# fp64 weights decoded by two parametric ReLUs and one VectorE pass instead of one scaling and three VectorE passes, with the rows loaded from their third byte on and the first stage put in another order

## The chip, the cores and the metric

The kernel runs on one core of a Trainium2 chip. The metric is the device time of one execution in microseconds (us). TensorE is called PE here, VectorE DVE, ScalarE ACT, GpSimd POOL, and SyncE, which issues nearly all transfers, SP.

## The reference, cut to what matters

Three blocks follow one another: an attention over 32 memory slots per head (8 batches of 576 tokens, 8 heads of 64), a feed-forward block with a squared ReLU (512 to 2048 to 512), and a second one with a softmax-gated unit and a layer norm (512 to 1024 to 512).

```python
a = softmax(phi)                      # over the 32 memory slots
k_m, v_m = a^T k, a^T v               # per batch and head
attn = softmax(q k_m^T / 8)           # over the 32 slots
x = (attn v_m)                        # 4608 tokens x 512
h = maximum(x @ w_in, 0);  x = (s * h * h + b) @ w_out
h = x @ w_in2;  x = layer_norm(h * softmax(h)) * g_ln @ w_out2
```

The four weight matrices come as 64-bit floating point (their scale factor is a 64-bit number), everything else as 32-bit. No engine computes in 64 bits, so the kernel builds a 32-bit float out of the bits of every weight. The first block's w_in (512x2048) and w_out (2048x512) are 8 MB each in that form.

## The kernel before, in words

Tokens lie batch after batch. The eight batches n = 0..7 are worked off in halves j = 0, 1 of 288 tokens. From batch 1 on the products run as pairs of 16-bit pieces. Batch 0 is a stage of its own, called FIRST, because it runs while the weights of the first feed-forward block are still being loaded and decoded; its first half uses 32-bit products.

**FIRST is a list of steps written out by hand** (lines 33 to 54 before the change): each name is a call, and the order of the names is the order in which every engine gets its instructions. Each engine works strictly in that order and waits where an operand or a buffer is missing. The names that matter here:

- Lphi, Lkv, Lq, Lw, Lo: loads on SP's queue, of phi, of k and v, of q, of a piece of w_in, of a piece of w_out. A piece is 128 partitions by 1024 weights, 1 MB; w_in is eight pieces c.x (c is the quarter of 512 columns, x the half of the rows), w_out another eight.
- Ai/Ao, Ci/Co, PiX/PoX: the three decoding steps of a piece of w_in or w_out. Before the change Ai (line 281) reads the upper 32-bit word of each weight as a float and multiplies it by 2^-112 on ACT; Ci (lines 285 and 286) shifts left by three and puts the sign back, two DVE passes; PiX (line 1201) fetches three more bits from the lower word, one DVE pass. Bi/Bo (line 294) then sums the piece's squares or absolute values on ACT.
- qm, qo: q of two heads is transposed on PE (line 561) and copied out on ACT (line 573). km, ks, ko: the memory products of k and v (lines 472 and 497) and their normalization. mm, mv, mk: their transposes and copies.
- s0, s1, s2, s3, s6, at, aA: scores of two of the six token chunks (line 844), softmax on DVE and ACT (lines 856 to 877), transposes back on PE (line 906), copy on ACT (line 914).
- vm, vA/vD: v_m times a quarter of w_in (line 609) and the copy out of PSUM (line 919).
- g, gr, gs: first products of batch 0 (line 927, four 32-bit products of 288 columns a step), ReLU (line 1035) and square (line 944) on ACT. Before g can start, two chunks' at/aA and one quarter's vm/vA have to be done.
- y and Y: second products of batch 0 (lines 955 and 1106).

PSUM tiles named h (tq, kp, sp, wp, ta, tx, hp) share three buffers, so a product can also wait until ACT or DVE has emptied an earlier tile. KEEP (line 58) is a table of filler products on PE (line 163) that are put in front of a step and whose result is not used. After FIRST comes the loop over n = 1..7, whose first product is line 1024. The change does not touch that loop.

Of the kernel before, what the change touches and what calls it, by code (L numbers as in the profile page):

```python
# [28 lines left out]
REBIAS = 2.0 ** -112  # L29
# [35 lines left out]
def tile_mem_attention__moe_relu2__solu_ln(  # L65
# [15 lines left out]
    nc = tc.nc  # L81
# [15 lines left out]
    scale = 1.0 / float(D) ** 0.5  # L97

    const = ctx.enter_context(tc.tile_pool(name="const", bufs=1))
# [17 lines left out]
    xiv = const.tile([128, NT // GRP], FP32)  # L117
    nhalf = const.tile([128, 1], FP32)
    half = const.tile([128, 1], FP32)
    rsc = const.tile([128, 1], FP32)  # L120
    sb = const.tile([128, 2], FP32)
    s22 = const.tile([128, 1], FP32)
# [4 lines left out]
    iw = const.tile([128, KD], FP32)  # L127
# [3 lines left out]
    gl = const.tile([128, KF2], FP32)  # L131
# [91 lines left out]
    def pow2_scale(al, inv, tag="sc", w=1):  # L223
# [915 lines left out]
    raw_t, pk_t = {}, {}  # L1139

    def load_w_in(f, kp, t):
        src = w_in.bitcast(I32)[kp * 256:(kp + 1) * 256, f * 1024:(f + 1) * 1024]
        nc.sync.dma_start(
            out=t.rearrange("p k f w -> p k (f w)"), in_=src.rearrange("(k p) f -> p k f", p=128)
        )
        raw_t["in", f, kp] = t

# [3 lines left out]
    def load_w_out(d, x):  # L1151
        if x == 0:
            t = w_out_t[d].rearrange("p a k d -> p (a k d)").bitcast(I32)
        else:
            t = raw_p.tile([128, 2048], I32, tag="raw", name="raw")
        rows = w_out.bitcast(I32)[x * 1024:(x + 1) * 1024, d * 256:(d + 1) * 256]
        nc.sync.dma_start(
            out=t.rearrange("p (k d) -> p k d", k=8), in_=rows.rearrange("(k p) d -> p k d", p=128)
        )
        raw_t["out", d, x] = t.rearrange("p (a x w) -> p a x w", a=2, w=2)  # L1160

# [21 lines left out]
    def piece_abs(w, c, x):  # L1183
        if w == "o":
            at = (2 * c + x) % 4
            wt_t[c, x] = wt_s[:, at] if at < 3 else flat(r2_s)[:, 0:1024]
        decode_rebias(*piece(w, c, x))

    def piece_low(w, c, x, eng):
        decode_low(raw_t["in" if w == "i" else "out", c, x], eng)  # L1190

    def piece_bits(w, c, x):
        decode_shift(*piece(w, c, x))

    def piece_add(w, c, x):
        decode_add(*piece(w, c, x))
# [375 lines left out]
    with tc.manual_schedule():  # L1572
        make_identity(nc, ident)
        nc.vector.memset(ones, 1.0)
        nc.vector.memset(nhalf, -0.5)
        nc.vector.memset(half, 0.5)
        nc.vector.memset(c15, 2.0 ** -15)
# [105 lines left out]
```

## Time and profile before

| | |
|---|---|
| median of two runs | 1087.83 us (1087.77 to 1087.89) |
| the profiled execution | 1088.45 us, of which 1086.7 us are the span from the first to the last instruction |
| PE busy | 1058.0 us, 97% of the span |
| DVE, ACT, POOL busy | 766.1, 527.4, 170.7 us |
| moved by DMA | 129.22 MB |

The profiled execution is 0.62 us longer than the median of the runs, and 1.75 us of it lie outside the span. PE's 28.7 idle us are the difference of its busy time and the span. The page cuts the span into 40 slices of 27 us; PE's digits there begin 5, 7 and stand at 9 nearly everywhere after that, and the DMA digits begin 9, 8, 9 and then fall to 5.

### The profile page before, as it was taken

The page shows a single profiled execution, that of the slowest core. Times are in us where ns is not written, and L with a number is a line of the kernel's source. Part 1 is how long each engine was busy: PE and PEld are TensorE (multiplying, and loading weights), DVE is VectorE, ACT ScalarE, POOL GpSimd, SP SyncE. Part 2 cuts the span into 40 slices and gives each one's busy share as a digit, 9 for nine tenths or more (in the row PEclk, how much of TensorE's full clock was granted, in tenths as well). Part 3 has the DMA queues.
Part 4 walks back from the last instruction along what each step waited for, and adds up shares of the span by engine and source line. Part 5 has one row for each costly group of instructions (what it writes and reads, how often), then busy time and mean ns, then how long its engine had stood idle before and what let it go on. Part 6 is the DMA issues. An engine that isn't in the chain of part 4 may idle for free.

```text
span 1086.7 us, 20776 instructions
## 1 busy us (share of the span) xinstructions
PE 1058.0 (97%) x8439; PEld 698.6 (64%) x8439; DVE 766.1 (71%) x1499; ACT 527.4 (49%) x775; POOL 170.7 (16%) x141
## 2 busy tenths in 40 slices
PE   5799999989999999999999999999999999999998
PEld 4577777767777777777777777754444444444443
DVE  4799988768768767767767766467766666666662
ACT  3689754654553553663653655423333333333322
POOL 0000200130120130120120110023122222221221
PEclk9999999999999999999999999999999999999999
DMA  9894535524725625636625152125443443434325
GB/s 295 271 256 137 126 108 108 134 60 121 177 64 134 166 61 134 167 61 163 167 60 124 27 185 63 32 58 119 105 107 88 113 105 94 107 95 110 88 59 107
DMA packets 208607, 129.22 MB, mean 119 GB/s; under 512 B 137344, under 2 KB 196736, under 8 KB 208512
## 3 DMA queue, kind: packets, MB, share of 16 engines
q1 hardware_dynamic: 208368, 127.70, 45.9%
q8 instruction: 66, 1.08, 0.4%
q14 instruction: 29, 0.24, 0.1%
q10 hardware_dynamic: 112, 0.20, 0.1%
q0 software_dynamic: 32, 0.00, 0.0%
HBM read 71.83 MB, written 23.07 MB: 87 GB/s over the span
## 4 chain that ended last, share of the span: by engine, by line
PE 88%; DVE 4%; DMA 3%; ACT 2%; POOL 1%; issue 1%; SPq 0%; POOLq 0%; ACTq 0%; DVEq 0%
PE y L1106 29%; PE y L1510 17%; PE hp L1428 17%; PE hp L1024 14%; PE hp L927 3%; PE y L955 3%; PE kp L472 2%; DMA q_s<-in_q_dram 2%; PE wp L651 1%; PE sp L800 1%; DMA work<-in_moe_w_out_dram 1%; DMA wt_s<-in_v_dram 1%; PE wp L609 1%; PE tq L561 1%; POOL e L877 0%
## 5 line engine op out<-in xcount | busy, mean ns | idle before, releaser
L1106 PE MATMUL y<-g,w_out 128*128 128x288 f16 x2688 | 338.5, 286 | 0.0
L1106 PEld LDWEIGHTS <-w_out 128*128 128x128 f16 x2880 | 278.1, 98 | 85.4 <-issue 11.0
L1428 PE MATMUL hp<-w_t,xs 128*128 128x512 f16 x864 | 192.0, 379 | 0.0
L1510 PE MATMUL y<-w_t,lt 128*128 128x512 f16 x864 | 191.7, 379 | 0.0
L1024 PE MATMUL hp<-aT,vwt 128*128 128x288 f16 x1344 | 167.6, 286 | 3.9 <-ACT r L1035 3.9
L1024 PEld LDWEIGHTS <-vwt 128*128 128x128 f16 x1344 | 131.4, 98 | 37.8 <-issue 4.6
L1510 PEld LDWEIGHTS <-lt 128*128 128x128 f16 x864 | 84.6, 98 | 101.7
L1428 PEld LDWEIGHTS <-xs 128*128 128x128 f16 x864 | 84.5, 98 | 101.4
L1472 POOL TENSOR_TENSOR rstd<-ve,nhalf 128x1 f32<-128x1 f32 x36 | 52.6, 1462 | 332.8 <-DVE mv L1470 332.8
L1442 DVE TENSOR_REDUCE hmx<-hp 128x1 f32<-128x1024 f32 x36 | 44.1, 1224 | 84.1 <-PE hp L1428 84.1
L314 ACT ACTIVATE xs<-xt,xsc 128x512 f16<-128x512 f32 x36 | 25.9, 720 | 151.3 <-PE hp L1428 129.9
L1123 ACT ACTIVATE x<-y,bcol,cs 128x288 f32<-128x288 f32 x60 | 35.1, 586 | 109.4 <-PE y L1106 99.8
L1089 DVE TENSOR_TENSOR g<-r_s,g 128x576 f16<-128x576 f32 x112 | 85.3, 762 | 3.8
L1082 ACT ACTIVATE r_s<-r 128x576 f32<-128x576 f32 x112 | 76.6, 684 | 16.8 <-DVE g L1089 13.6
L1035 ACT ACTIVATE r<-hp 128x576 f32<-128x576 f32 x120 | 77.3, 644 | 13.9 <-PE hp L1024 6.9
L1009 DVE CAST g<-r_s 128x576 f16<-128x576 f32 x112 | 51.5, 460 | 24.4 <-ACT r_s L1082 24.2
L1449 ACT ACTIVATE e<-hp,nm,xiv 128x1024 f32<-128x1024 f32 x36 | 43.3, 1202 | 45.6 <-DVE nm L1444 45.6
L311 DVE TENSOR_REDUCE xmx<-x 128x1 f32<-128x288 f32 x64 | 28.8, 450 | 50.6 <-ACT x L1123 50.2
L1518 ACT ACTIVATE o<-y,io 128x512 f32<-128x512 f32 x36 | 24.7, 687 | 53.0 <-issue 40.5
L1486 DVE TENSOR_TENSOR nat<-so,nat 128x1024 f16<-128x1024 f32 x36 | 43.8, 1216 | 5.4 <-ACT nat L1481 5.4
L1465 DVE BATCH_NORM_STATS2 bs<-so 128x6 f32<-128x512 f32 x72 | 46.3, 685 | 1.3
L1460 DVE SCALAR_TENSOR_TENSOR so<-hp,sm,e 128x1024 f32<-128x1024 f32 x36 | 46.2, 1284 | 1.3
(242 smaller groups left out, 1194.2 us busy)
## 6 DMA issues: line engine op xcount, KB each, us to landing
x_d<-x SPq DMA_DIRECT2D x64, 144.0 KB, 2.0
xt<-x_d SPq DMA_DIRECT2D x36, 256.0 KB, 3.1
kv_s<-in_k_dram SPq DMA_DIRECT2D x31, 288.0 KB, 6.6
kv_s<-in_v_dram SPq DMA_DIRECT2D x31, 288.0 KB, 7.2
q_s<-in_q_dram SPq DMA_DIRECT2D x21, 288.0 KB, 4.7
phi_sb<-in_phi_dram SPq DMA_DIRECT2D x8, 576.0 KB, 4.9
out_dram<-o SPq DMA_DIRECT2D x23, 192.0 KB, 2.6
w_out<-in_moe_w_in_dram SPq DMA_DIRECT2D x4, 1024.0 KB, 16.0
```

The lines of the kernel that those rows point to most:

```text
L1009: nc.vector.tensor_copy(out=g_of(n, j, 0)[:, 2 * fp:2 * fp + 2, 0:BLK], in_=gt["r2", j, fp])
L1024: nc.tensor.matmul(out=hp[:, u, 0:BLK], lhsT=vt[:, pw, R, f * 128:(f + 1) * 128], rhs=aT[:, CJ * j:CJ * (j + 1), pa, R, :], start=(x == 0) ...
L1035: nc.scalar.activation(out=r, in_=gt.pop(("h", j, fp))[:, :, 0:BLK], func=ACTF.Relu, scale=scale)
L1082: nc.scalar.activation(out=r2, in_=r, func=ACTF.Square)
L1089: (nc.vector if eng == "D" else nc.gpsimd).tensor_tensor(out=g_of(n, j, 1)[:, fs, 0:BLK], in0=gt.pop(("r2", j, fp)), in1=g_of(n, j, 0)[:, ...
L1106: nc.tensor.matmul(out=y[:, 0:w], lhsT=w_out_t[d][:, pw, f, :], rhs=g_of(n, j, pg)[:, f, 0:w], start=(x == 0), stop=(x == len(steps) - 1),)
L1428: nc.tensor.matmul(out=hp[:, a, :], lhsT=xs[:, px, kk, :], rhs=wt[:, pw, kk, a * 512:(a + 1) * 512], start=(kk == 0 and px == 0 and pw == ...
L1442: nc.vector.tensor_reduce(out=mx, in_=hv, op=ALU.max, axis=AX)
L1460: nc.vector.scalar_tensor_tensor(out=so, in0=hv, scalar=sm[:, 0:1], in1=e, op0=ALU.mult, op1=ALU.mult)
L1465: nc.vector.bn_stats(out=bs[:, a, :], in_=so[:, a * 512:(a + 1) * 512])
L1472: nc.gpsimd.tensor_tensor(out=rstd, in0=ve, in1=nhalf, op=ALU.pow)
L1510: nc.tensor.matmul(out=y[:, 0:DM], lhsT=lt[:, pl, f, :], rhs=wt[:, pw, f, :], start=(x == 0), stop=(x == len(steps) - 1),)
```

## The change

The source of a weight's row is now read as 16-bit words, starting with the second one, so every row lacks its first two bytes and each weight lies two bytes lower in the piece. Its top 16 bits (sign, exponent, four bits of mantissa) are then the third half-word of its eight bytes. Ai became a parametric ReLU on ACT that reads that half-word as an integer, with a bias and a slope of 2^60 for negative numbers; Ci became a second one that writes integers, with another bias and a slope of 2^-60; together they put the exponent and the sign in place. PiX shifts by 13 instead of 29 and brings the other 19 bits. So ACT has two passes for a piece where it had one, and DVE one where it had three. One copy of two numbers went from DVE to ACT. FIRST has a new order, and KEEP a new table (42 fillers instead of 25).

```diff
-Lphi.0 phm.0 Lkv.00 pht.0 phd.0 Lkv.01 pho.0 phb.00 phe.00 km.00 Lkv.03 Lkv.02 ks.00 phb.01 phe.01 km.01 ks.01 ko.00
...
+Lphi.0 phm.0 pht.0 phd.0 Lq.00 pho.0 phb.00 Lq.01 qm.00 Lkv.03 qm.01 qo.00 phe.00 Lkv.00 qo.01 Lq.02 phb.01 Lkv.01
...
 KEEP = {
-    "pht.0": 3, "km.00": 3, "mm.0": 3, "qm.02": 2, "qm.03": 1, "s0.00": 1, "vap.0": 1, "s0.02": 1, "at.1": 9,
-    "pho.1": 1,
+    "pht.0": 3, "km.00": 1, "vap.0": 1, "qm.02": 6, "qm.01": 3, "qm.00": 6, "s0.00": 1, "pht.1": 4, "at.1": 4,
+    "at.0": 2, "g.01": 9, "g.05": 1, "at.2": 4,
 }
-    def decode_rebias(dst, raw):
-        nc.scalar.activation(out=dst, in_=raw[:, :, :, 1].bitcast(FP32), func=ACTF.Copy, scale=REBIAS)
-
-    def decode_shift(dst, raw):
-        di = dst.bitcast(I32)
-        nc.vector.tensor_scalar(out=di, in0=di, scalar1=3, scalar2=None, op0=ALU.logical_shift_left)
-        nc.vector.scalar_tensor_tensor(
-            out=di, in0=raw[:, :, :, 1], scalar=-0x80000000, in1=di, op0=ALU.bitwise_and, op1=ALU.bitwise_or,
+    def decode_knee(dst, raw):
+        nc.scalar.activation(
+            out=dst, in_=raw.bitcast(I16)[:, :, :, 2], func=ACTF.Prelu, bias=knee[:, 0:1], scale=1.0, alpha=2.0 ** 60,
+        )
+
+    def decode_place(dst, raw):
+        nc.scalar.activation(
+            out=dst.bitcast(I32), in_=dst, func=ACTF.Prelu, bias=knee[:, 1:2], scale=2.0 ** 19, alpha=2.0 ** -60,
         )
     def load_w_in(f, kp, t):
-        src = w_in.bitcast(I32)[kp * 256:(kp + 1) * 256, f * 1024:(f + 1) * 1024]
+        src = w_in.bitcast(I16)[kp * 256:(kp + 1) * 256, f * 2048 + 1:(f + 1) * 2048]
...
-        rows = w_out.bitcast(I32)[x * 1024:(x + 1) * 1024, d * 256:(d + 1) * 256]
+        rows = w_out.bitcast(I16)[x * 1024:(x + 1) * 1024, d * 512 + 1:(d + 1) * 512]
...
-            out=dst.bitcast(I32), in0=raw[:, :, :, 0], scalar=29, in1=dst.bitcast(I32),
+            out=dst.bitcast(I32), in0=raw[:, :, :, 0], scalar=13, in1=dst.bitcast(I32),
             op0=ALU.logical_shift_right, op1=ALU.bitwise_or,
...
-        nc.vector.tensor_copy(out=iw[:, 2 * d:2 * d + 2], in_=inv.to_broadcast([128, 2]))
+        nc.scalar.copy(out=iw[:, 2 * d:2 * d + 2], in_=inv.to_broadcast([128, 2]))
```

Three places show what the new order does; line numbers of the changed kernel are two higher from line 83 on (and six higher at the end of the file). On SP, the loads at the start of the program, before (phi_sb, kv_s, q_s are phi, k and v, q; wt_s holds one more of either; the tiles whose source is in_moe_w_in_dram receive w_in):

```order
L332 DMA phi_sb<-in_phi_dram 96x8x192
L357 DMA kv_s<-in_k_dram 96x2x384
...
L357 DMA kv_s<-in_v_dram 96x2x384
L1143 DMA raw_g<-in_moe_w_in_dram 128x2x1024
L1143 DMA raw<-in_moe_w_in_dram 128x2x1024
L1143 DMA raw_g<-in_moe_w_in_dram 128x2x1024
L366 DMA wt_s<-in_q_dram 96x2x384
L1143 DMA raw<-in_moe_w_in_dram 128x2x1024
L366 DMA q_s<-in_q_dram 96x2x384 x3
L332 DMA phi_sb<-in_phi_dram 96x8x192
```

and in the changed kernel:

```order
L334 DMA phi_sb<-in_phi_dram 96x8x192
L368 DMA q_s<-in_q_dram 96x2x384 x2
L359 DMA wt_s<-in_k_dram 96x2x384
L359 DMA wt_s<-in_v_dram 96x2x384
L359 DMA kv_s<-in_k_dram 96x2x384
L359 DMA kv_s<-in_v_dram 96x2x384
L368 DMA q_s<-in_q_dram 96x2x384
...
L368 DMA wt_s<-in_q_dram 96x2x384
L1145 DMA raw_g<-in_moe_w_in_dram 128x2x2047 x2
L1145 DMA raw<-in_moe_w_in_dram 128x2x2047 x2
```

All four pieces of q now go ahead of all w_in, where before four pieces of w_in went ahead of three of q. On PE, the same stretch of the changed kernel after the first filler products (tq is a transpose of q, kp the memory products, sp scores, ta a transpose of the softmax, wp the product with w_in, hp the first real product of batch 0):

```order
L423 MATMUL tx<-first 96x256
...
L563 MATMUL tq<-ident,q_s 64x96 x12
...
L563 MATMUL tq<-ident,q_s 64x96 x12
...
L563 MATMUL tq<-ident,q_s 64x96 x12
...
L474 MATMUL kp<-kv_s,phi_sb 32x128 x24
...
L563 MATMUL tq<-ident,wt_s 64x96 x12
L541 MATMUL tp<-ident,km 128x128 x2
...
L846 MATMUL sp<-kmT,qt_s 96x2x32 x24
```

Before, the memory products came first and each score product behind the transposes of all of q. Ahead of the three tq groups now stand 6, 3 and 6 fillers. On ACT, what stood between the first scaling of a piece and the first exponential before:

```order
L281 ACTIVATE w_in_t<-raw_g 128x2x512
L546 COPY first<-tp 64x128 x2
L281 ACTIVATE w_in_t<-raw 128x2x512
L550 COPY kmT<-tp 64x4x32 x2
L281 ACTIVATE w_in_t<-raw_g 128x2x512
L294 ACTIVATE junk,pk<-w_in_t 128x1024
L281 ACTIVATE w_in_t<-raw 128x2x512
L573 COPY qt_s<-tq 128x576 x3
```

and now, from the first parametric ReLU on:

```order
L283 ACTIVATE w_in_t<-raw_g,knee 128x2x512
L548 COPY first<-tp 64x128 x2
L288 ACTIVATE w_in_t<-w_in_t,knee 128x2x512
L865 ACTIVATE e<-e 96x512 x2
L283 ACTIVATE w_in_t<-raw_g,knee 128x2x512
L288 ACTIVATE w_in_t<-w_in_t,knee 128x2x512
L296 ACTIVATE junk,pk<-w_in_t 128x1024
L865 ACTIVATE e<-e 96x512
L283 ACTIVATE w_in_t<-raw,knee 128x2x512
L916 COPY aT_119<-ta 128x2x192
L288 ACTIVATE w_in_t<-w_in_t,knee 128x2x512
L296 ACTIVATE junk,pk<-w_in_t 128x1024
```

The exponentials of the scores and the copies that PE waits for now stand between the decoding passes of w_in, where before four pieces had been scaled ahead of the first exponential.

## Rows read from the trace of the kernel before

**Rows 1.** Windows by stage: start:end, length, busy us (instructions) per engine, clock, DMA.

```profile
0.00:50.00 50.00, 31.93 (x414) 24.18 (x415) 30.41 (x56) 22.56 (x34) 0.68 (x6) 1.00 1.00 306
50.00:110.00 60.00, 60.00 (x465) 45.27 (x464) 56.94 (x108) 55.30 (x84) 1.00 (x1) 1.00 0.66 181
...
150.00:1087.00 937.00, 926.08 (x7232) 599.20 (x7229) 640.41 (x1270) 424.60 (x624) 163.00 (x131) 1.00 0.43 106
```

**Rows 2.** Chain of waits, 0 to 200 us: start, us, what; xN counts two records a product.

```profile
12.18 17.10 DMA q_s<-in_q_dram
...
29.32 4.11 PE tq L561 x48
33.43 1.89 PE wp L609 x16
...
49.88 5.88 PE hp L927 x24
55.76 1.43 PE kp L472 x46
57.19 0.47 PE kp L497 x39
57.66 1.02 PE wp L609 x16
...
71.70 3.90 PE y L955 x16
...
150.66 11.78 PE hp L1024 x96
```

**Rows 3.** Timeline of PE, 0 to 62 us: start, us, what, count, idle before.

```profile
10.17 0.85 PE L163 MATMUL kp<-first 128*128 128x256 f16 x3
12.30 2.89 PE L472 MATMUL kp<-kv_s,phi_sb 96*32 96x128 f32 x48 [1.28 <-ACT phi_sb L449]
...
43.67 1.16 PE L163 MATMUL ta<-first 128*128 128x256 f16 x9
...
46.52 0.59 PE L421 MATMUL tx<-first 128*96 128x256 f32 x2
```

**Rows 4.** Timeline of ACT, 33 to 46 us.

```profile
38.36 1.07 ACT L294 ACTIVATE junk<-w_in_t 128x1024 bf16<-128x1024 f32 x1
...
39.55 1.06 ACT L294 ACTIVATE junk<-w_in_t 128x1024 bf16<-128x1024 f32 x1
...
42.33 0.63 ACT L863 ACTIVATE e<-e 96x512 f32<-96x512 f32 x1 [1.62 <-DVE e L858]
42.86 1.28 ACT L281 ACTIVATE w_in_t<-w_out 128x1024 f32<-128x1024 f32 x1
```

**Rows 5.** Groups by line and shape, DVE, 0 to 240 us: busy us, mean ns, idle.

```profile
L285 DVE TENSOR_SCALAR w_in_t<-w_in_t 128x1024 int32<-128x1024 int32 x8 | 5.5, 686 | 0.0
...
L286 DVE SCALAR_TENSOR_TENSOR w_in_t<-w_out,w_in_t 128x1024 int32<-128x1024 int32 x4 | 4.9, 1225 | 0.1
...
L1201 DVE SCALAR_TENSOR_TENSOR w_in_t<-w_out,w_in_t 128x1024 int32<-128x1024 int32 x4 | 4.8, 1219 | 0.0
```

**Rows 6.** The same view, ACT.

```profile
L1035 ACT ACTIVATE r<-hp 128x576 f32<-128x576 f32 x25 | 16.2, 647 | 3.6 <-PE hp L1024 1.7 <-PE hp L927 0.7
...
L314 ACT ACTIVATE w_out<-wt_s,sc 128x1024 f16<-128x1024 f32 x6 | 6.8, 1137 | 0.0
...
L1035 ACT ACTIVATE r<-hp,rsc 128x576 f32<-128x576 f32 x8 | 5.8, 725 | 0.2 <-DVE rsc L1039 0.2
...
L281 ACT ACTIVATE w_in_t<-w_out 128x1024 f32<-128x1024 f32 x4 | 4.7, 1181 | 0.0
...
L914 ACT COPY aT<-ta 128x384 f32<-128x384 f32 x3 | 1.4, 470 | 0.4 <-PE ta L906 0.4
```

**Rows 7.** Windows in which k, v, phi load, and in which w_in loads.

```profile
4.00:10.00 6.00, 1.34 (x4) 0.83 (x5) 2.58 (x5) 1.28 (x1) 0.00 (x0) 1.00 1.09 268
33.00:38.00 5.00, 4.30 (x46) 2.22 (x42) 0.19 (x1) 2.33 (x5) 0.00 (x0) 1.00 1.02 404
```

More of the change, by code (lines that the diff above doesn't have):

```diff
@@ L12 @@
 I32 = mybir.dt.int32
+I16 = mybir.dt.int16
 U32 = mybir.dt.uint32
@@ new lines @@
+qm.02 Lkv.02 km.00 phe.01 ks.00 Lq.03 Lw.00 km.01 qo.02 ks.01 ko.00 ko.01 qm.03 vb.0 vad.0 mm.0 mk.0 qo.03 vap.0 s0.00
+Ai.00 s0.01 mv.0 s1.00 s1.01 Ci.00 PiX.00 s2.00 Lw.01 s3.00 Lw.10 s6.00 s2.01 s0.02 Ai.01 at.0 s1.02 Ci.01 Bi.00 Lw.11
+s3.01 PiX.01 s2.02 Ai.10 aA.0 vm.00 Ci.10 s3.02 Lw.21 s6.01 at.1 Bi.01 vA.00 PiX.10 Ai.11 aA.1 vD.01 g.01 Lw.20 Lphi.1
+Ci.11 PiX.11 vm.01 Bi.10 Ai.21 Bi.11 va.0 s6.02 at.2 Ci.21 Lw.30 gr.01 PiX.21 Ai.20 vA.10 Ci.20 g.00 gr.00 phm.1 vA.11
+aA.2 gs.0 PiX.20 gs.1 Bi.20 pht.1 vm.02 phd.1 pho.1 g.03 vA.20 vA.21 g.04 Bi.21 phb.11 phe.11 phb.10 phe.10 gr.03
@@ new lines @@
+Lkv.10 Lkv.11 km.10 gr.04 Ai.30 gs.3 Lw.31 Ci.30 g.02 gr.02 ks.10 Ai.31 Ci.31 PiX.30 ko.10 g.05 gs.4 Lkv.13 PiX.31
+vm.03 Lkv.12 Lsb km.11 Lo.00 Bi.30 gr.05 Lo.01 ks.11 ko.11 mb.1 vA.30 mad.1 Lo.11 vA.31 Lo.10 gs.2 Bi.31 g.06 im iad
+g.07 vb.1 gs.5 Ao.00 Lq.11 gr.06 Lq.10 iap Co.00 map.1 Ao.01 vad.1 g.11 Lo.30 ia PoX.00 gr.07 Bo.00 gs.7 g.14 Ao.11
+gs.6 Co.01 ma.1 Ao.10 iv vs.0 PoX.01 vr vap.1 g.13 Co.11 Co.10 Lq.13 Bo.01 y.00 y.01 gr.11 qa.10 PoX.11 PoX.10 va.1
+Lq.12 vs.1 Bo.11 Bo.10 cb.0 yo.00 gh.1 qa.13 gr.14 g.10 om.0 oad.0 gq.1 oap.0 oa.0 Lo.20 os.0 gh.4 xh.00 gl.1 Lo.21
@@ new lines @@
+qa.12 y.10 ym.00 xh.01 gq.4 gr.13 Lphi.2 y.11 xl.00 gl.4 Ao.20 gr.10 xl.01 qa.11 qs.1 gh.3 Co.20 cb.1 yo.01 xh.10
+PoX.20 ym.01 xl.10 Lo.31 phm.2 Ao.21 xh.11 Co.21 mm.1 Ao.30 qh.11 g.12 PoX.21 g.15 gq.3 xl.11 mv.1 gl.3 y.20 Co.30
+ql.11 y.21 PoX.30 ms.1 cc.0 Ao.31 yd.00 gr.12 Co.31 PoX.31 mh.1 qh.10 ql.10 pha.2 gh.0 ml.1 yd.01 gh.2 Bo.20 Bo.21
+gq.0 mT.1 g.17 cb.2 gq.2 g.16 qT.10 gl.2 yo.02 gl.0 Bo.31 y.30 gr.15 y.31 cb.3 Bo.30 gr.17 om.1 oad.1 yo.03 vm.12
+qT.11 ym.02 qh.12 qh.13 gh.5 gq.5 vm.10 vh.10 oap.1 gh.7 vh.12 ql.12 ql.13 oa.1 qT.13 Y.00 gl.5 os.1 ym.03 gr.16
@@ L54 @@
+phbP.2 vl.10 vl.12 gq.7 gl.7 qT.12 gh.6 Y.10 gq.6 gl.6 s0.10 sc.10 s0.11 xh.30 s1.10 sc.11 xl.30 xh.20 Y.01 s2.10
+xl.20 s0.12 cc.1 yd.02 xh.31 xh.21 Lkv.21 Y.11 yo.10 yo.11 s3.10 s1.11 s6.10 ym.11 s2.11 Lkv.20 s3.11 s6.11 s4.10
+s5.10 yd.03 s4.11 vm.11 xl.31 Y.30 ym.10 vh.11 vm.13 xl.21 s5.11 sT.10 yd.10 Y.20 vh.13 sT.11 sc.12 yd.11 s1.12 vl.11
+Y.31 Y.21 Lq.21 yo.13 s2.12 s3.12 ym.13 s6.12 phe.2 vl.13 yd.13 s4.12 s5.12 Lkv.22 Lq.20 yo.12 ym.12 Lq.22 yd.12 sT.12
 """
 KEEP = {
[L59 removed]
@@ L119, in tile_mem_attention__moe_relu2__solu_ln @@
     half = const.tile([128, 1], FP32)
+    knee = const.tile([128, 2], FP32)
     rsc = const.tile([128, 1], FP32)
@@ L1141, in load_w_in @@
     def load_w_in(f, kp, t):
-        src = w_in.bitcast(I32)[kp * 256:(kp + 1) * 256, f * 1024:(f + 1) * 1024]
+        src = w_in.bitcast(I16)[kp * 256:(kp + 1) * 256, f * 2048 + 1:(f + 1) * 2048]
         nc.sync.dma_start(
-            out=t.rearrange("p k f w -> p k (f w)"), in_=src.rearrange("(k p) f -> p k f", p=128)
+            out=t.rearrange("p k f w -> p k (f w)").bitcast(I16)[:, :, 0:2047],
+            in_=src.rearrange("(k p) f -> p k f", p=128),
         )
@@ L1155, in load_w_out @@
             t = raw_p.tile([128, 2048], I32, tag="raw", name="raw")
-        rows = w_out.bitcast(I32)[x * 1024:(x + 1) * 1024, d * 256:(d + 1) * 256]
+        rows = w_out.bitcast(I16)[x * 1024:(x + 1) * 1024, d * 512 + 1:(d + 1) * 512]
         nc.sync.dma_start(
-            out=t.rearrange("p (k d) -> p k d", k=8), in_=rows.rearrange("(k p) d -> p k d", p=128)
+            out=t.rearrange("p (k d) -> p k d", k=8).bitcast(I16)[:, :, 0:511],
+            in_=rows.rearrange("(k p) d -> p k d", p=128),
         )
@@ L1186, in piece_abs @@
             wt_t[c, x] = wt_s[:, at] if at < 3 else flat(r2_s)[:, 0:1024]
-        decode_rebias(*piece(w, c, x))
+        decode_knee(*piece(w, c, x))
     def piece_low(w, c, x, eng):
@@ L1192, in piece_bits @@
     def piece_bits(w, c, x):
-        decode_shift(*piece(w, c, x))
+        decode_place(*piece(w, c, x))
     def piece_add(w, c, x):
@@ L1576, in tile_mem_attention__moe_relu2__solu_ln @@
         nc.vector.memset(half, 0.5)
+        nc.vector.memset(knee[:, 0:1], 14336.0)
+        nc.vector.memset(knee[:, 1:2], -28672.0 * 2 ** 19)
         nc.vector.memset(c15, 2.0 ** -15)
```

19 lines of the change are left out of this document (removed).

## The prediction, written before the change was run

> **What bounds the kernel now.** I read the windows by stage first. From 50 us on PE hardly idles: 60.00 of 60 us between 50 and 110, and 926 of 937 us after 150 [rows 1]. Only the first 50 us hold idle time that an order of steps could remove: PE is busy for 31.9 of them. DVE and ACT are nearly full between 50 and 110 (56.9 and 55.3 of 60 us), yet PE does not wait for them there. So taking passes off DVE is worth nothing after 50 us. What counts is when PE's unbroken work begins, and whether it stays unbroken.
>
> The chain of waits says what sets that beginning. The last piece of q lands 17.1 us after its issue at 12.18; only then come its transposes, scores, softmax and back-transposes, and the first product of batch 0 (line 927) starts at 49.88. From there the chain is PE down to the loop's first product (line 1024) at 150.66 [rows 2]. The loop's code is untouched, so I carry a shift of that 150.66 to the end one for one.
>
> A third thing to see is PE's speed. The eight products of a line 609 group take 1.89 us at 33.43 and 1.02 at 57.66 [rows 2]; three fillers take 0.85 at 10.17, nine take 1.16 at 43.67 [rows 3]. So PE runs at the lower of its two levels at first and at the higher by 43.67. The clock column says 1.00 in all windows [rows 1], also where products run at half speed; I go by the durations. The rise came during the first unbroken stretch, 8 us long, that begins at 29.32 [rows 2].
>
> **Part 1, the earlier start.** phi is loaded first in both versions, so PE's fillers begin at 10.2 again [rows 3]. In the new order 15 fillers and three transposes of q follow. A filler of 256 columns takes 0.2 us at the lower level (three in 0.85 with the last one's run-out), one of 208 columns 0.17, so 15 take 2.6; a transpose group takes 4.11 / 2 = 2.05 [rows 2], three 6.2. That ends at 19.0. By then PE has worked 8 us without a break, as long as before its rise, so I take the higher level from here: two memory products of 1.43 + 0.47 [rows 2] end at 22.8, the fourth transpose (half of 2.05) at 23.8, and with normalization, transpose and copies the scores start at about 24.6.
>
> Now ACT decides. From its first parametric ReLU at 24.8 up to the second copy aA, which the first product needs, it has four first passes, three second passes, two sums, three exponentials, three copies of about 0.45 (470 ns less overlap, [rows 6]) and two small copies of together 0.5. For a parametric ReLU the trace has no row. The nearest ones: the same shape with one pointer operand, 1137 ns, and the strided scaling that it replaces, 1181 ns without a pointer, whose price is 725 - 647 = 78 ns [rows 6]. Back to back an ACT pass hides about 0.1 us: two exponential and scaling passes start 0.53 apart where the first takes 0.63 [rows 4]. So I take 1.15 for a first pass and 1.04 for a second; the bounds are 0.96 (the sum's 1.06 less overlap, [rows 4]) and 1.28 (the longest scaling, [rows 4]) for either. A sum takes 1.19 (38.36 to 39.55, [rows 4]), an exponential 0.53. That is 4 x 1.15 + 3 x 1.04 + 2 x 1.19 + 3 x 0.53 + 3 x 0.45 + 0.5 = 13.5, and about 1.1 of waits for DVE's softmax passes between the exponentials. The first product then starts at 24.8 + 14.6 = 39.4 instead of 49.88: **-10.5 us**.
>
> **Part 2, work that moves behind that start.** Batch 1's two small phi products stood before 49.88 and now come later: 0.59 for the larger [rows 3], 0.9 together. Nine fillers (at.2, pht.1, g.05) stand behind the start: 1.16 for nine [rows 3], so 1.0 without run-out. **+1.9 us**. The nine of g.01 and six of at.0 and at.1 run while PE waits for ACT and cost nothing as long as it does; if ACT were earlier they would cost up to 1.7.
>
> **Part 3, new waits.** After the start ACT's queue is full, and three h buffers tie PE to it.
> - The second product step needs a buffer that the first one's ReLU frees. Between aA and that ReLU stand two second passes, two sums and one first pass and the rest of aA: 2 x 1.04 + 2 x 1.19 + 1.15 = 5.6, so the ReLU ends near 45.5. PE has 1.96 (5.88 / 3, [rows 2]) + 1.02 + 0.8 of other work, to 43.2. Wait 2.3.
> - The next h tile needs the second ReLU, behind one first pass, one copy and one second pass: it ends at 48.8, PE is done at 47.5. Wait 1.3.
> - Batch 1's memory products wait for exponentials of phi in the same queue: 0.7.
> - The last quarter of w_in: from 24.8 ACT has 36.4 us of passes up to its last second pass (8 x 1.15 + 8 x 1.04 + 6 x 1.19 + 11.8 of exponentials, copies, ReLUs and squares) and 2 to 3 us of waits, so 63; DVE's one pass (1.22, [rows 5]) ends at 64.0. PE comes there at 39.4 + 17.6 of work (six steps of 1.96, two groups of 1.02, 1.90 of memory products, part 2's 1.9) + 4.3 of waits + half a group = 61.9. Wait 2.1.
>
> Together **+6.4 us**. Behind that w_out's pieces are loaded and decoded well ahead of their products, and nothing waits.
>
> **Edits I cost at nothing.** DVE loses 16 x (0.69 + 1.23 us) less overlap [rows 5], some 28 us; its cover is that PE does not wait for DVE after 50 us. The moved copy is one small pass on ACT in a stretch where PE is full; without that cover it costs a few tenths. The transfers keep their bytes. A piece of w_in takes 1.05 MB / 404 GB/s = 2.6 us [rows 7] and ACT takes one every 4 us, so 1 us more for each is hidden. Rows that start two bytes late appear nowhere in the trace; from below I see no gain in them, from above I take the slower of the two rates in the trace, 268 against 404 GB/s [rows 7], 1.5 times as long. I take no difference, since rows keep their length and number. The Trainium skill says as much (DMA: Bandwidth & Descriptors, How a descriptor splits into AXI transactions): a descriptor that starts off a 256 B boundary begins at the boundary below it, which for a row from byte 2 to byte 4096 adds no transaction; no run here shows it.
>
> **Sum.** -10.5 + 1.9 + 6.4 = -2.2: line 1024 starts near 148.5, the profiled execution takes 1088.45 - 2.2 = 1086.3. That execution stands 0.62 above the median, so I predict **1085.6 us**.
>
> **Rivals.**
> - *Slower: the clock stays low until w_in's products.* Memory products with 32 columns ran at the lower level from 12 to 18 us without lifting it. If the fillers do not lift it either, it rises at about 37. Then two memory products take 2.89 instead of 1.43 less run-out [rows 2, 3], 2.6 together, the fourth transpose 1.0 and the rest 0.8: +4.4, so 1090.0. It decides if the rise comes after about 22 us: every microsecond of delay costs about half of one, and the gain is gone.
> - *ACT becomes the bound of the whole stage.* Between 50 and 110 it has 55.3 of 60 us [rows 1] and gets eight more second passes, 8.3 us, less some 4.8 of sums of w_in that now come before 50. If each remaining pass ends up ahead of a ReLU, the overload of about 4 us shows as PE's waits: 1089.6. The Trainium skill's rule speaks for it (ScalarE: Activation LUTs, Rules for kernel authors): ReLU, maximum, addition and multiplication belong on VectorE, which is the faster engine for them. By the rows one pass on ACT replaces 1.9 us on DVE, so here the rule holds only for the engine that ends up full.
> - *The odd rows are slow.* At 1.5 times as long w_out's eight pieces take 3.9 us each, as much as a part of line 955 (3.90, [rows 2]), and w_in's come 1.3 later each: about +5, 1091. Twice as long would cost w_out 8 x 1.3 more and w_in its cover, over 20 us in all.
> - *Faster: the clock is up at about 14* instead of 19, which saves half of two transposes and of some fillers, 2.5, and ACT's passes are at their lower bound, which shortens Part 1 by 1: 1082.
>
> **Chances.** Forecast (1084 to 1088.5) 0.48; clock late 0.20; ACT bound 0.12; odd rows 0.08; faster 0.12. The range **1082 to 1092** holds the forecast with its bounds, both slower cases of PE and ACT, and half of the other two. A change of 2%, 21.8 us, is about what a measurement of this kernel can tell from none. No case is that much faster (0.01); of the odd rows a quarter would be that much slower (0.02); within 2%: 0.97.
>
> **What the profile would show.** Part 1 is right if line 929 (was 927) starts at 38 to 41 and the three tq groups stand between 10 and 19. Part 3 is right if ACT has almost no idle time between 25 and 64 and PE's waits there name ACT's ReLU, about 6 us in all; if they are under 3 the time is nearer 1082. The clock shows in line 474's groups: 1.4 us each or 2.6. Odd rows show in the landing times of w_in's loads (12 to 16 us before) and in waits of ACT for DMA. I would be wrong altogether if PE idled after 64 us, or if the loop's first product and the end did not shift by the same amount.

## The result, and the profile after

The changed kernel takes 1100.48 us (two runs, 1099.93 and 1101.03) against 1087.83: 1.0116 times as long, with a 95% interval of 1.0073 to 1.0160. Timed again beside the experiments it took 1.0093 times as long (1.0078 to 1.0109). So it is about 1% slower, 10 to 12.6 us, where the prediction had 2.2 us faster and a range that ended at 1092. The profiled execution took 1099.93 us with a span of 1098.2.

The windows by stage show the shape at once. The columns are those of [rows 1]: the stretch, busy us of PE, PEld, DVE, ACT and POOL, the granted clock, the DMA share, GB/s.

```profile
0.00:50.00 50.00, 33.37 (x436) 24.29 (x436) 21.40 (x49) 24.87 (x36) 0.68 (x6) 0.86 0.99 286
50.00:110.00 60.00, 51.74 (x404) 37.20 (x405) 31.38 (x77) 50.03 (x73) 0.57 (x1) 0.97 0.82 194
163.00:1098.00 935.00, 927.32 (x7230) 599.50 (x7227) 642.38 (x1274) 424.30 (x626) 163.53 (x131) 1.00 0.45 106
```

Up to 50 us PE is busier than before (33.4 against 31.9 us). Between 50 and 110, where it was full, it now idles for 8.3 us, while DVE's work has fallen from 56.9 [rows 1] to 31.4. Behind that nothing is new. The chain of waits, which before was PE without a break from 49.88 on [rows 2], now leaves PE for ACT and for two loads:

```profile
11.89 2.00 PE tq L563 x24
...
14.27 1.14 PE tq L563 x24
...
17.41 1.43 PE kp L474 x46
...
19.30 1.06 PE kp L474 x29
20.36 3.10 issue
23.46 0.71 PE kp L474 x16
...
25.17 2.12 PE tq L563 x24
...
58.69 1.47 ACT phi_sb L451 x2
...
64.56 9.78 DMA w_out<-in_moe_w_out_dram
...
78.70 17.89 DMA kv_s<-in_q_dram
96.62 0.95 DVE qmx L313
...
98.50 9.50 PE y L957 x32
...
163.37 11.76 PE hp L1026 x96
```

Four things are to be read here. PE's speed rose early: a group of q's transposes takes 2.00 us at 11.89 and 1.14 at 14.27. Then, in the middle of the second group of memory products, PE stands still for 3.10 us; "issue" means that it waited for nothing that the profile shows. Behind that the same transposes take 2.12 us again. From 38.3 to 60.2 us nearly every piece of the chain is a pass on ACT; the row at 58.69 is the last of them. And at 78.70 a load of q takes 17.89 us to land, a reduction on DVE waits for it, and PE waits for what stands behind that reduction. The loop's first product, line 1026, starts at 163.37 where it was 150.66 [rows 2]: +12.7 us. The span grew by 11.5.

PE's timeline gives the first product of batch 0 (line 929; line 927 was at 49.72 in this view) and the stall:

```profile
44.88 2.13 PE L929 MATMUL hp<-aT,vw 128*128 128x288 f32 x8
...
92.39 2.21 PE L929 MATMUL hp<-aT,vw 128*128 128x288 f32 x8 [1.94 <-ACT r L1037]
98.01 0.49 PE L196 MATMUL mp<-first 128*128 128x128 f32 x2 [3.42 <-DVE first L190]
```

The wait of 1.94 us is for a ReLU on ACT (line 1037) that stands behind decoding passes, one of which had waited for a piece of w_out; the wait of 3.42 us is for what stands behind the reduction of q on DVE. ACT's timeline:

```profile
87.36 1.23 ACT L283 ACTIVATE wt_s<-w_out,knee 128x1024 f32<-128x1024 int16 x1 [2.40 <-DMA w_out<-in_moe_w_out_dram]
...
91.61 0.72 ACT L1037 ACTIVATE r<-hp,rsc 128x576 f32<-128x576 f32 x1
```

Now the view of who waited for whom, for PE from that first product to the loop's (total, times, longest):

```profile
PE hp L929 <- ACT r L1037: 3.6, 2, 1.9
PE mp L196 <- DVE first L190: 3.4, 1, 3.4
PE sp L802 <- DMA work<-kv_s: 1.4, 1, 1.4
PE wp L611 <- DVE w_in_t L1205: 1.0, 1, 1.0
PE tx L165 <- ACT r L1037: 1.0, 1, 1.0
PE y L957 <- DVE rsc L1041: 0.2, 1, 0.2
```

That is 10.6 us of waits in a stretch that had none before. By PE's timeline the stretch is 118.3 us long (44.88 to 163.21) and was 100.8 (49.72 to 150.53):

```profile
49.72 6.04 PE L927 MATMUL hp<-aT,vw 128*128 128x288 f32 x24
```

Less the waits, PE's work in it has grown by 6.9 us. By groups and lines, PE in the same stretch after, with four of the rows:

```profile
L611 PE MATMUL wp<-w_in_t,first 64*32 64x512 f32 x48 | 4.3, 600 | 1.1 <-DVE w_in_t L1205 1.0
...
L423 PE MATMUL tx<-first 128*96 128x256 f32 x2 | 0.7, 418 | 0.0
L165 PE MATMUL ta<-first 128*128 128x256 f16 x4 | 0.6, 276 | 0.0
L165 PE MATMUL tx<-first 128*128 128x256 f16 x4 | 0.6, 272 | 1.0 <-ACT r L1037 1.0
```

and before, the answering row of line 609:

```profile
L609 PE MATMUL wp<-w_in_t,first 64*32 64x512 f32 x32 | 2.2, 601 | 0.0
```

A third product group of v_m with w_in now stands behind the start (4.3 against 2.2 us), the fillers and batch 1's phi products bring 2.5 more (the rows shown, and two of 0.3), and the first two parts of line 957 after the stall take 9.50 us where a part took 3.90 [rows 2], 1.7 more. The granted clock was 0.62 between 98.5 and 103 us. That is 6.3 of the 6.9. The account of the +12.7: start -4.8, work +6.9, waits +10.6.

Why q landed so late is on SP's queue. Its timeline in the changed kernel (issues of transfers; the time is that of issuing):

```profile
34.64 2.44 SPq L1145 DMA_DIRECT2D w_out<-in_moe_w_in_dram  x1
61.75 0.31 SPq L359 DMA_DIRECT2D kv_s<-in_k_dram  x1
...
64.56 0.43 SPq L1160 DMA_DIRECT2D w_out<-in_moe_w_out_dram  x1
...
78.70 6.77 SPq L368 DMA_DIRECT2D kv_s<-in_q_dram  x2
```

For 25 us, from 37 to 61.75, SP issues nothing. At its head stands a load of batch 1's k into a buffer that the memory products at 60.21 free. Behind it stand all eight pieces of w_out, whose first was issued at 36.50 before. From 64.56 to 98 they and q then share the DMA engines.

### The profile page after: what moved, and what is told of

It is laid out like the page before. It is cut to its first block, busy times and chain, and to the rows that moved or that the text cites. A ratio compares the mean times of both kernels' runs of the same rounds, so it can differ in the third digit from the quotient of the medians.

```text
span 1098.2 us, 20786 instructions
## 1 busy us (share of the span) xinstructions
PE 1064.0 (97%) x8459; PEld 699.4 (64%) x8459; DVE 738.5 (67%) x1467; ACT 541.7 (49%) x793; POOL 170.8 (16%) x141
## 4 chain that ended last, share of the span: by engine, by line
PE 86%; DVE 4%; DMA 4%; ACT 3%; issue 1%; SPq 0%; POOL 0%; ACTq 0%; POOLq 0%; DVEq 0%
PE y L1108 29%; PE y L1514 17%; PE hp L1432 17%; PE hp L1026 14%; PE y L957 2%; PE kp L474 2%; DMA kv_s<-in_q_dram 2%; PE wp L653 1%; PE sp L802 1%; DMA w_out<-in_moe_w_out_dram 1%; PE hp L929 1%; DMA work<-in_moe_w_out_dram 1%; PE tq L563 1%; DMA phi_sb<-in_phi_dram 0%; DVE w_in_t L319 0%
## 5 line engine op out<-in xcount | busy, mean ns | idle before, releaser
L1108 PEld LDWEIGHTS <-w_out 128*128 128x128 f16 x2880 | 278.4, 98 | 86.3 <-issue 11.5
L1011 DVE CAST g<-r_s 128x576 f16<-128x576 f32 x112 | 51.5, 460 | 23.0 <-ACT r_s L1084 22.8
L1453 ACT ACTIVATE e<-hp,nm,xiv 128x1024 f32<-128x1024 f32 x36 | 43.3, 1202 | 45.5 <-DVE nm L1448 45.5
```

What stands on the lines that cost most here:

```text
L1011: nc.vector.tensor_copy(out=g_of(n, j, 0)[:, 2 * fp:2 * fp + 2, 0:BLK], in_=gt["r2", j, fp])
L1108: nc.tensor.matmul(out=y[:, 0:w], lhsT=w_out_t[d][:, pw, f, :], rhs=g_of(n, j, pg)[:, f, 0:w], start=(x == 0), stop=(x == len(steps) - 1),)
```

## The experiments

Theory O says that the new order costs the time, theory R that the odd rows do, theory A that ACT does with its second pass; theories named later stand with their run. Times are given as ratios to the kernel before, timed on the same chip. "First product" is line 929 or its equal, "loop" the start of the loop's first product, by PE's timeline; the same readings are 49.7 and 150.5 us before, and 44.9 and 163.2 after.

### Rows, order and decoding apart

**Whole rows.**

```diff
-        src = w_in.bitcast(I16)[..., f * 2048 + 1:(f + 1) * 2048]
+        src = w_in.bitcast(I16)[..., f * 2048:(f + 1) * 2048]
-        rows = w_out.bitcast(I16)[..., d * 512 + 1:(d + 1) * 512]
+        rows = w_out.bitcast(I16)[..., d * 512:(d + 1) * 512]
-            ... in_=raw.bitcast(I16)[:, :, :, 2], ...
+            ... in_=raw.bitcast(I16)[:, :, :, 3], ...
```

> The changed kernel with w_in's and w_out's rows loaded whole again, from their first byte on, and the first decoding pass reading the fourth half-word instead of the third; the low 19 bits of every mantissa are then not the reference's. Theory R (odd rows load slowly): w_out's loads land about 2 us sooner after their issue (13.4 us instead of 15.6), PE's idle stretch between 85 and 98 us shrinks by half or more, about 1093 to 1096. Theory O (the order of the loads and steps costs it, whatever the rows): landing times as in the changed kernel, ratio to it within 0.2%, about 1100. Theory A (ACT is full): 1100 too.

Measured: 1.0075 (1.0045 to 1.0105), which overlaps the 1.0093 of the changed kernel. The median times from issue to landing of w_in's loads are about the same; with whole rows:

```profile
w_out<-in_moe_w_in_dram SPq DMA_DIRECT2D x4, 1024.0 KB, 17.7
raw_g<-in_moe_w_in_dram SPq DMA_DIRECT2D x2, 1024.0 KB, 13.0
raw<-in_moe_w_in_dram SPq DMA_DIRECT2D x2, 1024.0 KB, 15.5
```

and with odd rows 17.9, 12.3 and 15.2. w_out's two groups of loads land in 14.7 and 13.9 us with whole rows, in 15.6 and 15.3 in the changed kernel and in 14.3 and 14.2 in its second trace. In the next run, with the old order, odd rows land even in 9.6 and 10.1 us, where whole rows took 13.4 and 14.7 before the change. Theory R falls.

**New decoding, old order.**

```diff
-FIRST, KEEP of the changed kernel
+FIRST, KEEP of the kernel before
```

> The new decoding with odd rows, but with the list of steps and the table of fillers of the kernel before. Theory O: w_out's loads are issued at 36 to 62 us again, PE does not idle between 85 and 98 us; 1086 to 1091, since ACT's second passes come where PE waits little. Theory A: ACT, full from 50 to 110 before, gets 16 second passes of 1.15 us, PE waits for its ReLUs, 1096 or more. Theory R: w_out's landings stay at 15 us and more, PE waits for them, 1093 or more.

Measured: 1.0114 (1.0092 to 1.0137), first product 50.8, loop 163.6. PE does not stall at 85 to 98 us, yet this is as slow as the changed kernel: theory O alone falls as well. PE's waits behind the first product now name DVE's last decoding pass,

```profile
PE y L957 <- DVE wt_s L1205: 3.0, 2, 2.7
PE wp L611 <- DVE w_in_t L1205: 2.2, 1, 2.2
```

which itself comes behind ACT's second pass in that decoding: for it DVE idles 19.3 us ahead of w_in's pieces and 6.6 ahead of w_out's. That is theory A's sign. Of the 13.1 us by which the loop starts later, 1.0 is the later first product and 5.7 are idle time of PE behind it. For the other 6.4 PE is busy longer, in part at a lower clock (granted 0.57 from 70 to 74 us and 0.83 from 120 to 130); I did not divide them up further.

**Old decoding, new order.**

```diff
-FIRST, KEEP of the kernel before
+FIRST, KEEP of the changed kernel
```

> The decoding and the whole rows of the kernel before with the new list of steps and the new table of fillers. Theory O: w_out's loads are again issued only from about 60 us on, PE idles for 5 us or more between 80 and 105 us, 1096 or more. Theory A or R: without the second passes on ACT and with whole rows the stall is gone and the earlier first product shows: 1083 to 1088.

Measured: 1.0195 (1.0171 to 1.0219), first product 52.7, loop 174.2. Theory O's time came, not its sign: w_out is issued from 76.8 us on, but PE idles for only 1.7 us between 80 and 105. From the first product to the loop it waits 10.7 us, 8.8 of them for DVE. Of the four pairs of order and decoding, the two that were changed alone are 1.0114 and 1.0195, both together 1.0093. With the old order the new decoding costs 1.1%; with the new order it saves 1.0%. Neither can be priced by itself: with the new decoding DVE's last pass waits for ACT, with the old one PE waits for DVE's own longer queue.

### The stall at 90 to 98 us

**w_out's first two loads ahead of the waiting load.**

```diff
-... gs.4 Lkv.13 PiX.31 vm.03 Lkv.12 Lsb km.11 Lo.00 Bi.30 gr.05 Lo.01 ...
+... gs.4 Lo.01 Lo.00 Lkv.13 PiX.31 vm.03 Lkv.12 Lsb km.11 Bi.30 gr.05 ...
```

> The changed kernel with one edit of the list: the loads of w_out's pieces 0.1 and 0.0 stand ahead of the third pair of batch 1's k and v loads instead of behind the fourth. Theory O: the first piece is issued near 42 us instead of 65, the second near 55, all eight land earlier, the idle stretch at 85 to 98 us shrinks from 6 us to 2 or less, 1092 to 1096. Theory R: the loads still take longer and DVE still waits for them: 1098 to 1101. Theory A: no change, 1100.

Measured: 1.0047 (1.0034 to 1.0060), the loop at 155.8. That is 7.4 us sooner than in the first trace of the changed kernel and 4.9 sooner than in its second (below); by the ratios the edit brings 5.0 us. PE is busy for every us from 70 to 130, and its waits from the first product to the loop are down to 3.6 us:

```profile
PE tx L165 <- ACT r L1037: 1.0, 1, 1.0
PE wp L611 <- DVE w_in_t L1205: 1.0, 1, 1.0
PE sp L802 <- DMA work<-kv_s: 0.9, 1, 0.9
PE hp L929 <- ACT r L1037: 0.6, 1, 0.6
```

Theory O holds for this part of the loss. The edit does two things, though: w_out comes earlier, and so does q behind it (its last two issues begin at 73.7 instead of 78.7).

**DVE's reductions of q moved back, loads as in the change.**

```diff
-... Bo.01 y.00 y.01 gr.11 qa.10 PoX.11 PoX.10 va.1 Lq.12 ... gh.1 qa.13 gr.14 g.10 om.0 ... gl.1 Lo.21 qa.12 ...
+... Bo.01 y.00 y.01 gr.11 PoX.11 PoX.10 va.1 qa.10 Lq.12 ... gh.1 gr.14 g.10 om.0 ... gl.1 Lo.21 qa.13 qa.12 ...
```

> The changed kernel with w_out's loads where the change put them, but with the two reductions of batch 1's q, for which DVE waited 3.75 us at 90 and 1.83 us at 96.6 us, moved behind the decoding of w_out's second pair and behind w_out's scale. Theory H (the stall at 92 to 98 us is DVE's queue, held at its head by a load of q): PE's wait of 3.4 us for line 190 goes, 1094 to 1096. Rival (it is w_out's own pieces that come late): PE idles 4 us or more between 85 and 100 us all the same, 1097 to 1100.

Measured: 1.0063 (1.0044 to 1.0082); the profiled execution has the loop at 156.1. PE's wait for line 190 is 0.4 us instead of 3.4. w_out's loads are issued as late as in the change (from 65.28 us on), so their place did not make that wait: it was DVE's queue, with a reduction of q at its head and w_out's scale, for which PE waited, behind it. The other wait, 1.94 us for ACT's ReLU, is gone as well, though the edit moves nothing on ACT; w_out's two groups of loads landed in 12.7 and 13.7 us here instead of 15.6 and 15.3, and this execution was the shortest of its four. In their profiles either cure takes away nearly all of the stall; by the ratios this one brings 3.3 us and the other 5.0.

### The late start

**Fillers over PE's pause.** On top of the run with w_out's two loads ahead, as all that follow.

```diff
-    "km.00": 1, "vap.0": 1,
+    "km.00": 1, "km.01": 28, "vap.0": 1,
```

> The run with w_out's two loads ahead, and 28 more filler products on PE in front of the second group of batch 0's memory products, which fill the 3 us in which PE waits there for the last k and v. Theory C (that idle stretch lets PE's clock fall to its lower level, and the scores and what follows pay double): the group of the last k and v ends within 1 us of before, the 48 score records take about 2.8 us instead of 5.3, line 929 starts 2 to 4 us sooner (42 to 44 us), 1089 to 1091. Rival (the start is bound by ACT's passes or by the loads, not by PE's speed): line 929 starts within 1 us of that run, or later because the fillers stand in PE's way, 1093 to 1094.

Measured: 1.0059 (1.0044 to 1.0074), first product 46.7. The pause is covered and the second group of memory products runs at the higher level, but PE then stops for 1.2 us after three records of the scores, again for nothing that the profile names, and the 48 records take 4.5 us. Theory C's gain does not appear, though its condition, the scores at full speed, was not reached either.

**Half of w_in decoded as before.**

```diff
+            if f >= 2: whole rows
-        decode_knee(*piece(w, c, x))
+        (decode_rebias if w == "i" and c >= 2 else decode_knee)(*piece(w, c, x))
-        decode_place(*piece(w, c, x))
+        (decode_shift if w == "i" and c >= 2 else decode_place)(*piece(w, c, x))
...
+            ... scalar=29 if w == "i" and c >= 2 else 13, ...
```

> The run with w_out's two loads ahead, with the third and fourth quarter of w_in loaded and decoded as in the kernel before (whole rows, one pass on ACT and three on DVE), the rest with the two parametric ReLUs. Theory A (what is left is ACT, which is full from 34 to 73 us): four second passes of 1.15 us less on ACT, PE's waits for ACT's ReLUs and for the last quarter of w_in between 50 and 70 us (3 us in all) shrink to 1 or less, 1090 to 1091.5. Rival (DVE's 8 us more come in the way, or the waits were not ACT's): 1093 or more.

Measured: 1.0107 (1.0090 to 1.0124), loop at 163.1, 7.4 us later than without the edit (6.5 by the ratios). The rival was right. PE now waits for small DVE steps that stand behind DVE's extra passes:

```profile
PE wp L621 <- DVE rs L523: 2.4, 1, 2.4
PE tx L412 <- DVE pm L403: 1.8, 1, 1.8
```

**Both together.**

```diff
+    "km.01": 28,
+    the old decoding for w_in's third and fourth quarter
```

> Both edits, the 28 fillers and the old decoding for half of w_in, with w_out's two loads ahead. Theories C and A together: the two gains add, 1086 to 1089. Rival: one of them takes the other's place, since an earlier first product finds ACT just as full, 1090 or more.

Measured: 1.0129 (1.0107 to 1.0152). The rival's time came, but not for its reason: neither gain had appeared alone, and PE waits for the same two DVE steps as in the run before (2.4 and 1.8 us).

**The changed kernel once more.**

```diff
 no edit
```

> The changed kernel itself once more, unchanged, for its size on the chip of these runs: 1099 to 1101, line 929 near 45 us, PE idle for 5 to 6 us between 85 and 98 us.

Measured: 1.0093 (1.0078 to 1.0109); first product 45.9, the wait for line 190 2.2 us, the loop at 160.7. PE idles for 3.0 us between 85 and 98 us, less than expected, and the granted clock behind the stall stays at 1.00 (98 to 103 us). So the size of the stall, and whether the clock falls behind it, differ between executions of the same kernel.

**k and v ahead of all q.**

```diff
-Lphi.0 phm.0 pht.0 phd.0 Lq.00 pho.0 phb.00 Lq.01 qm.00 Lkv.03 ...
+Lphi.0 phm.0 pht.0 phd.0 Lkv.03 Lkv.00 Lkv.01 Lkv.02 Lq.00 pho.0 phb.00 Lq.01 qm.00 ...
```

> The run with w_out's two loads ahead, and batch 0's eight k and v loads ahead of all q at the start of the program. Theory L (the first product waits for the last byte of phi, k, v and q, 4.1 MB that land at 200 to 230 GB/s, so their sequence does not matter): the last of them lands near 25 us as before, line 929 starts within 1 us of 46.5, 1092 to 1095. Rival (the sequence matters, because k and v first would let the memory products run while q lands): line 929 starts 2 us or more sooner, 1091 or less; or 2 us or more later, since the transposes of q stand ahead of the memory products on PE, 1096 or more.

Measured: 1.0092 (1.0072 to 1.0112), first product 54.0. The rival was right: the sequence matters. PE waits 5.9 us for the first q, and the first product comes 7.5 us later. The loads of k and v are also not what the pause waits for. Here they are loaded ahead of everything but phi, and the chain of waits still shows the pause at the same place, behind records that have read all tiles of the group:

```profile
27.00 1.06 PE kp L474 x30
28.07 2.14 issue
30.21 0.90 PE kp L474 x15
```

**Fewer fillers behind the start.**

```diff
-    "pht.1": 4, ..., "g.05": 1, "at.2": 4,
```

> The run with w_out's two loads ahead, without the nine fillers that stand behind the first product (four at at.2, four at pht.1, one at g.05). As the prediction had it: 1.0 us less, 1092. Rival (PE waits for ACT there, so their time comes back as a longer wait): no difference, 1093.

Measured: 1.0049 (1.0033 to 1.0066), against 1.0047 with them. The rival: their time comes back as a wait (2.0 us for ACT's ReLU ahead of line 929, where it was 0.6).

**Squares on DVE.**

```diff
-        nc.scalar.activation(out=g32_of(fp // 4)[...], in_=gt.pop(("r", 0, fp)), func=ACTF.Square)
+        r = gt.pop(("r", 0, fp))
+        nc.vector.tensor_tensor(out=g32_of(fp // 4)[...], in0=r, in1=r, op=ALU.mult)
```

> The run with w_out's two loads ahead, with the eight squares of batch 0's first half (line 946) on DVE instead of ACT. Theory A (ACT, full from 34 to 73 us, makes PE's last 3 us of waits between 50 and 70 us): 5.4 us less on ACT, the waits fall to 1 us or less, 1090.5 to 1091.5. Rival (ACT and DVE wait for each other in turn, and DVE's queue then holds the squares ahead of what PE waits for): 1093 or more.

Measured: 1.0058 (1.0043 to 1.0074). The rival: the waits for ACT's ReLU grow from 1.6 to 2.5 us, and those for DVE's decoding from 1.0 to 1.9.

**No early fillers.**

```diff
-    "qm.02": 6, "qm.01": 3, "qm.00": 6,
```

> The run with w_out's two loads ahead, without the 15 fillers that stand ahead of the first three groups of q's transposes. Theory P (PE's pause in the second group of memory products comes after a fixed number of instructions, while more of its code is fetched): the pause comes 7 or 8 products later in the group, after some 45 of its 48 records instead of 30. Rival (it waits for a load, or for a time): the pause stays at record 30. For the clock: with the early fillers gone it rises later, the transposes and memory products take twice as long, line 929 starts 0 to 2 us later, 1093 to 1096; if the early clock is worth nothing because the pause undoes it, 1091.5 to 1093.5.

Measured: 1.0047 (1.0032 to 1.0061), first product 45.2, not later than with them. PE now runs the transposes and the first group of memory products at the lower level (2.70 us for line 474 instead of 1.43), and the pause moves with the count of instructions:

```profile
20.89 2.59 PE kp L474 x43
23.48 0.84 issue
24.32 0.23 PE kp L474
```

43 records instead of 29. It ends at 24.3, where with the fillers it ended at 23.5 to 25.8 in the runs that load q first. So whatever PE gains before that point it loses in the pause.

**ACT's sums later, and everything together.**

```diff
-... aA.0 vm.00 ... at.1 Bi.01 vA.00 ...
+the eight Bi steps moved back, four of them behind gs.2
```

> The run with w_out's two loads ahead, with ACT's eight sums of w_in (1.2 us each) put later in the list: two fewer ahead of the copy that the first product needs, three fewer ahead of the last quarter's decoding. Theory A (ACT's queue sets the start and the waits up to 70 us): line 929 starts 1.5 to 2.4 us sooner, near 44.5, the last quarter of w_in comes 3 us sooner, 1090 to 1091.5. Rival (DVE or PE's own chain sets the start, and the sums then stand ahead of w_out's decoding): line 929 moves by less than 1 us, 1093 or more.

Measured: 1.0061 (1.0040 to 1.0082), first product 45.5. It moved by about 1 us, and PE then waits longer for line 1037 (1.7 us). The rival.

```diff
+the two reductions of q moved back as well
-    "at.1": 4,
```

> The run with the sums late, with batch 1's two q reductions behind w_out's decoding as well, and without the four fillers ahead of the second transpose of the softmax. If each of these is worth on its own what the traces say: 0.5 to 1 us less than the run with the sums late, 1089 to 1091; if PE has no other wait to lose between 70 and 130 us: the same time.

Measured: 1.0068 (1.0051 to 1.0086). No gain. No version beat the kernel before: an estimate for the run with w_out's two loads ahead, with every one of the 3.6 us of waits that are left in it removed (5.1 - 3.6), still stands 1.5 us above it.

## Why the prediction was wrong, step by step

**The step that failed first: "w_out's pieces are loaded and decoded well ahead of their products, and nothing waits."** It had no working. PE waits for 7.0 us behind 75 us where the prediction had nothing, and in that execution the clock falls once more; moving two loads brings 5.0 us back by the ratios, 4.9 to 7.4 by the traces. I had read SP's order at the start of the program and not where w_out stands in it. The list shows w_out behind a load into a buffer that is free only when batch 1's memory products are done; the prediction counted those products among PE's work up to 61.9 us and did not ask which loads wait for them. The prediction named its own undoing, PE idle after 64 us.

**The sizes.** The forecast for line 1024 was -2.2 and the trace has +12.7. The 14.9 us between them are 7.0 from these waits, 5.7 from Part 1, 2.7 from Part 2 and 2.3 from work that took longer, less 2.8 from Part 3. So without the stall the change would still not have been faster: with w_out's two loads ahead it is 1.0047.

**Part 1, -10.5, measured -4.8.** The clock rose at 14 us, earlier than the 19 I took, so that rival's first half came true. It gained nothing (without the early fillers the first product came no later), because PE paused from 20.36 to 23.46 and ran at the lower level behind. The memory products ended near 25 instead of 22.8, ACT's first parametric ReLU began at 29.03 instead of 24.8:

```profile
29.03 1.22 ACT L283 ACTIVATE w_in_t<-raw_g,knee 128x1024 f32<-128x1024 int16 x1
...
34.49 1.20 ACT L283 ACTIVATE w_in_t<-raw_g,knee 128x1024 f32<-128x1024 int16 x1
35.72 1.15 ACT L288 ACTIVATE w_in_t<-w_in_t,knee 128x1024 int32<-128x1024 f32 x1
36.78 1.04 ACT L296 ACTIVATE junk<-w_in_t 128x1024 bf16<-128x1024 f32 x1
```

The later begin is 4.2 us of what is missing. From there to the first product it took 15.9 us instead of 14.6, another 1.3. The prices were near: 1.23 from one start to the next for a first pass (1.15 taken) and 1.06 for a second (1.04 taken), inside the bounds. What would bring the start forward stays open: a covered pause, no early fillers and later sums all left the first product at 45 to 47 us.

**Part 2, +1.9, measured 4.6, and 2.3 more that work took longer,** of which 1.7 are line 957 at the lower clock and 0.6 are not divided up. I counted the fillers and the phi products (2.5 measured) and forgot a whole group of line 611 (2.1), which stood before the first product in the old order and stands behind it in the new one. The new table has 45 fillers, not the 42 given with the change: line 165 has 45 records where line 163 had 25.

**Part 3, +6.4, measured 3.6** up to 70 us: 1.6 for the second step's buffer, 1.0 and 1.0. ACT's queue was as full as forecast (19.3 us busy of the 20 from 50 to 70); PE came later to it.

**Edits at nothing.** Odd rows: right, by the whole-row run and by landing times that are about equal (w_in's 17.9, 12.3 and 15.2 us against 17.7, 13.0 and 15.5). The Trainium skill's rule (DMA: Bandwidth & Descriptors, How a descriptor splits into AXI transactions) agrees with these runs. DVE's relief: wrong as a principle. In the new order it is worth 11 us, ACT's second passes already paid (1.0195 with the old decoding against 1.0093), and giving half of w_in's share back cost 6.5. What the trace before showed, that PE does not wait for DVE, was true of that order alone.

**Rivals.** The low clock came, late and not early. ACT as the bound of the whole stage is not shown for the changed kernel: the chain does run over ACT from 38.3 to 60.2 us, but later sums, squares on DVE and half of the old decoding, which each relieve ACT there, brought nothing back. The waits point to it in the old order with the new decoding (1.0114). The Trainium skill's rule (ScalarE: Activation LUTs, Rules for kernel authors) fits that pair only. That rival's price was also loose: 8.3 - 4.8 is 3.5, not about 4, and with it ACT's 55.3 of 60 us would not have been overfull. The slower side as a whole had 0.40, and none of its cases was the one that happened.

**The carry of line 1026** was near: +12.7 there, +11.5 at the end.

## What to carry to other kernels

When a list of steps is rewritten, follow every queue to its end, the one that issues loads first: write down what stands at its head when each load is due, and what frees that buffer. A step that only reads a late load (here a reduction of 0.95 us) must not stand in an in-order queue ahead of something that the bounding engine waits for. And an order and the costs it was made for belong together: price a change of both with the four pairs, not as a sum of two changes.

## What the runs showed of the hardware

PE stopped for 0.8 to 3.6 us at a place that is fixed by the number of instructions before it: after 29 or 30 records of a group with the 15 fillers ahead, after 43 without them, also with k and v loaded ahead of q. With 28 more fillers ahead the group ran through in one run and stopped for 0.2 us after 2 records in the other, and both stopped again for 1.2 and 1.8 us after three records of the scores. In the changed kernel one packet of the queue that the profile calls "instruction" ran at about 21 us, in this pause, while the DMA share was 1.07. In every run with the new order such a packet starts 2 to 3 us before PE goes on: at about 21.0 for 23.46 in the changed kernel, 27.5 for 30.21 with k and v first, 21.75 for 24.32 without the early fillers, 28.5 for 30.91 with the 28 fillers. The Trainium skill (Runtime: NRT & Kernel Launch, Instruction fetch mechanics) says that a sequencer fetches its code in blocks over a DMA queue of its own, and that crossing a block is mostly hidden. The place agrees with blocks; if the pause is this fetch, it was not hidden in these runs. That the pause is this fetch is the likely reading and not shown: no run changed the fetch itself.

Behind this pause the granted clock fell from the higher level to the lower, though PE had gone back to work. In the changed kernel, where PE stood still for 3.10 us, the window behind it reads:

```profile
24.00:29.00 5.00, 5.00 (x88) 4.46 (x81) 1.40 (x6) 1.02 (x3) 0.00 (x0) 0.50 1.02 409
```

0.50 is the lower of the two levels, with PE busy for all 5 us. With w_out's loads late and q's reductions moved back the pause was 1.99 us, and the clock was 0.50 from 27 to 29 us. A stop of about that length did not always do it: behind the 2.15 us in which the changed kernel, run once more, waited for line 190, the clock stayed at 1.00. What decides between the two is not shown.
